# Routing's place in the order of a mixture-of-experts kernel, three weight loads, one turned block and the engines of the last two splits

## The chip, the cores and the metric

One core of a Trainium2 chip runs one program. The time is device microseconds of that core, the median of 3 runs. Engines: PE is TensorE, DVE is VectorE, ACT is ScalarE, POOL is GpSimd, SP is SyncE, whose queue issues nearly all transfers. Each engine works through its own list of instructions in order.

## The reference

Three steps follow each other. The input is 2304 tokens of 512 numbers (4 sequences of 576 positions, 8 heads of 64), all in float32.

```python
# 1 retention
scores = scale * np.matmul(q, k.transpose(0, 1, 3, 2))
out = np.matmul(scores * Dmat, v)              # Dmat: causal, gamma ** distance
# 2 mixture of experts, the best 2 of 8
noisy_logits = x @ w_gate + np.log1p(np.exp(x @ w_noise)) * noise
top2 = np.argpartition(-noisy_logits, 2, axis=1)[:, :2]
h = np.maximum(x[mask] @ w1[e], 0.0)           # 512 -> 1024
out[mask] += top2_w[mask, k, None] * (h @ w2[e])
# 3 feed-forward, 512 -> 2048 -> 512
h = x @ w_in
return ((h * np.cos(h)) @ w_out).astype(np.float32)
```

## The kernel before

**Float32 products in three passes.** Weights and activations are split into a high part `h` (rounded by ACT) and a low part `l` (the difference, by DVE or POOL), and a product is h·h + l·h + h·l (`PASSES`). Weights come as *units* of 128 x 1024 floats, 512 KB each. `load_unit` (L285) puts one transfer of a unit into SP's queue, into one of three staging tiles `st`. `split_unit` (L298) makes the high part on ACT (L308) and the low part on DVE or POOL (L309), and then calls `load_unit` for the next one. Units 0 to 3 are the first layer of expert 0, 4 to 7 its second layer.

**Stage A** (loop at L1000, 20 tiles of 128 tokens). Step `j` loads the q, k and v of tile j + 4 (1 MB), has POOL multiply q by the decay for tile j + 2 (`decay`, L449, `qt<-qr`), computes the scores of tile j + 1 (L475, L484), the outputs of tile j (L498 to L517) and the gate of tile j - 1, and writes the tile's rows to the buffer `xs` in DRAM (L543). From step 3 on (`WJ`), one unit of expert 0's first layer is split in each step.

**Routing** runs as generators in four groups of tiles (`routing`, L608). A generator yields after every operation or two. It computes softplus, the top 2 and a one-hot matrix on DVE (up to L671, `mm`), then running counts on PE (L678 to L687, the *ranking*), then for each tile two one-hot pairs on DVE (L718, L719) that PE multiplies into `ptab` (L710), a table of which token goes to which place of which expert. After the last group `rank_experts` (L565) sorts the experts by size: PE L579 and L580, then a chain on DVE from L740 to L751. The order also tells which expert's weights come next.

**Stage B.** While the last two groups are routed, PE computes expert 0 on its first 352 places, which were gathered from the first two groups alone: `layer1` (L892, 8 chunks of 12 matmuls) and `layer2` (L913, 4 chunks of 24, in two PSUM banks in turn; DVE turns each finished chunk into `y`, L918). The order is fixed when the program is built, by a planner of a few lines. It keeps two estimated clocks, `P` for the array's matmuls and `D` for routing, and `pump` (L945) takes the next routing operations as long as `D` is not more than `SLACK` = 1.8 ahead of `P`:

```python
for k, _ in enumerate(post):        # a step of stage B, three or so matmuls
    spent(0.33, L_US)               # P += 0.33; D counts L_US for DVE's share
    pump()
```

Afterwards POOL gathers the remaining rows of expert 0 (L811), PE transposes them (L859), a matmul spreads the indices (L560), the engines pass a branch on overflowing experts (L1079), and `layer1` of expert 0's remaining places begins (L892).

**Expert stretch** (L1387). Experts 0 to 7 follow each other; while one is computed, POOL gathers rows for the next and `turn(e + 1, blk)` (L847) brings them into columns. For expert 1, blocks 0 and 1 are *whole-row* blocks: ACT copies the rows into the one tile `xt` (L856), PE transposes it (L859), ACT and DVE split it (L836, L837). Other blocks are turned by DVE alone (L844). Within expert 0, `TURN_AT0` says behind which step of its second layer (24 matmuls a step) each block is turned.

**Last stage** (L1442). Nine blocks of 256 tokens: `mlp1` (L1329), cosine on ACT and DVE, `mlp2` (L1358). During the first block, the last units of w_out are split; PE uses the last two, d2 and d3, at the end of `mlp2`. `turn2` (L1280) prepares the next block: ACT and DVE combine two expert outputs with their weights (L1307, L1308), DVE transposes (L844), ACT and DVE split (L836, L837).

Of the kernel before, what the change touches and what calls it, by code (L numbers as in the profile page):

```python
# [48 lines left out]
ZERO = (22, 27, 27, 29, 33, 38, 44)  # L49
LOOK = 4  # L50
WJ = 3
T0_AT = ()
SP0 = (0, 1, 3, 5, 7, 9)

# [20 lines left out]
ONE2 = 0.7  # L75
MARK2 = -0.5
B_US = 1.1
L_US = 0.04
OP_US = 0.21
ONE_US = 0.7  # L80
MARK_US = 0
# [1 line left out]
SPLIT_POOL = False  # L83
L1_WAIT = 2
B_AT = (0, 5, 10, 24)
TURN_AT0 = (1, 1, 2, 3, 4)
GN = max(z - a for a, z in GRP)
EARLY_N = GRP[EARLY - 1][1] // NC * S + GRP[EARLY - 1][1] % NC * 128
MID = N // 2
# [127 lines left out]
def moe_kernel(ctx, tc, x, out, dbg=None, phases="ABC"):  # L217
    nc = tc.nc
# [12 lines left out]
    state = {}  # L231
# [33 lines left out]
    units = []  # L265
# [19 lines left out]
    def load_unit():  # L285
        u = state["load"]
        if u >= len(units):
            return
        if u // 8 < E and u // 8 not in expert:
            state["owed"] += 1  # L290
            return
        state["load"] += 1
        st = stage.tile([128, 1024], F32, name="st")
        src = units[u][1]
        nc.sync.dma_start(st, src() if callable(src) else src)
        loaded[u] = st

    def split_unit(lo_engine=nc.vector):  # L298
        u = state["split"]
        state["split"] += 1  # L300
        tag, _, shp = units[u]
        st = loaded.pop(u)
        if tag[0] == "x":
            hi, lo = (t.rearrange("p a b -> p (a b)")[:, :1024].rearrange("p (a b) -> p a b", a=DC)
                      for t in x_tiles(int(tag[1])))
        else:
            hi, lo = (state[tag[0]].tile(shp, F32R, name=k + tag) for k in "hl")
        nc.scalar.activation(hi.rearrange("p a b -> p (a b)"), st, AF.Copy)  # L308
        lo_engine.tensor_tensor(lo.rearrange("p a b -> p (a b)"), st,  # L309
                                hi.bitcast(F32).rearrange("p a b -> p (a b)"), op=OP.subtract)  # L310
        W[u] = (hi, lo)
        load_unit()


    A = ExitStack()
# [244 lines left out]
            nc.tensor.matmul(pq[:, g], state["spread"][:, g], src, start=True, stop=True)  # L560
        return pq

    ranked, begun = [0], []

    def rank_experts():  # L565

# [41 lines left out]
    def routing(gi):  # L608
# [98 lines left out]
        def table(keep, last=False):  # L707
            while len(sel) > keep:
                r, sa, sb = sel.pop(0)
                nc.tensor.matmul(ptab, sa[:r], sb[:r], start=not begun, stop=last and not sel,  # L710
                                 skip_group_check=True)
                begun.append(1)

        for c in range(n):
# [7 lines left out]
            yield "one"  # L722
            table(4)
        yield "table"
        table(0, gi == len(GRP) - 1)
        if gi == EARLY - 1:

# [88 lines left out]
    def pace(src):  # L816

        nc.gpsimd.tensor_copy(beat, src.bitcast(F32))  # L818
# [120 lines left out]
    def spent(pe, dve=0.0):  # L939

        at["P"] += pe
        if dve:
            at["D"] = max(at["D"], at["P"] + PE_LAT) + dve

    def pump():  # L945

        clock[0] += 1
        while at["D"] < at["P"] + (SLACK if l1 else SLACK2):
            for it in gens[:2] if l1 or not LASTFIRST else gens[1::-1]:
                if it[1] <= at["P"]:  # L950
                    break
            else:
                return
            m = next(it[0], "end")
            if m == "end":
                gens.remove(it)
            elif m == "wait":
                it[1] = at["P"] + 0.3
            elif m == "done" and not l1:

                gens.remove(it)
                rest.append(it)
            else:
                one, mark = (ONE_US, MARK_US) if l1 else (ONE2, MARK2)
                at["D"] = max(at["D"], at["P"]) + (one if m == "one" else OP_US)
                if m in ("rank", "table"):
                    it[1] = at["D"] + mark
                elif m == "one":
                    it[1] = at["D"] - 2 * one
# [30 lines left out]
    for j in range(-2, NTILE + 1):  # L1000
        if j >= 0:
            load_tile(j + LOOK)
        if j == WJ - 2:
            for _ in range(3):
                load_unit()
        if 0 <= j + 2 < NTILE:
            decay(j + 2)
        if j == -2:
            late = late_consts()
            next(late)  # L1010
        pump()
        tail = j % NC == NC - 1
        if 0 <= j + 1 < NTILE:
            decay_v(j + 1)
            for _ in scores(j + 1):
                spent(0.87 if (j + 1) % NC == NC - 1 else 0.5, 0.6)
                pump()
        if j >= -1:
            next(late, None)
        turn_early()  # L1020
        if 0 <= j - 1 < NTILE:
            gate(j - 1)
            spent(0.37, 0.6)
        pump()
        fill(LF[0])
        if 0 <= j < NTILE:
            outputs(j)
            spent(1.75 if tail else 2.8)
        fill(LF[1])
        pump()  # L1030
        turn_early()
        if 0 <= j - 1 < NTILE:
            gate_t(j - 1)
            spent(0.11, 0.13)
            for gi, (_, z) in enumerate(GRP):
                if z == j:
                    gens.append([routing(gi), 0])
        fill(LF[2])
        if j < NTILE:
            pump()  # L1040
        for i in range(7):
            if ZERO[i] == j:
                zero_overflow(i)
        if j >= WJ and state["split"] < 4:
            split_unit(nc.gpsimd if SPLIT_POOL else nc.vector)
            if not SPLIT_POOL:
                spent(0, 1.1)
    A.close()
# [4 lines left out]
        turned.append(1)  # L1053
    late, l1, post = [2], None, chain(l1, layer2(0, 0, True))
    for k, _ in enumerate(post):
        spent(0.33, L_US)
        pump()
        if k in T0_AT and not gens:
            turn(0, late[0])
            late[0] += 1  # L1060
        if k in B_AT:
            split_unit()
            spent(0, B_US)
        for i in range(7):
            if ZERO[i] == NTILE + k:
                zero_overflow(i)
# [304 lines left out]
    def steps(g, n):  # L1371
        for _ in range(n):
            next(g, None)
# [13 lines left out]
    for e in range(E):  # L1387
# [31 lines left out]
        for _ in chain(layer2(e, 0), layer2(e, 1)) if 0 < e < E - 1 else layer2(e, 1):  # L1419
# [7 lines left out]
            else:  # L1427
                for blk in range(NB):
                    if (TURN_AT if e else TURN_AT0)[blk] == m:
                        turn(e + 1, blk)  # L1430
# [11 lines left out]
    for i in range(len(blocks)):  # L1442
        parts = []
        n = 0
        fg = fetch(i + 1)
        for _ in mlp1(i, parts):
            if n in SP0 and state["split"] < len(units):
                split_unit()
            if not i and parts:
                pace(parts[-1][0][0:1, 0, 0:1])  # L1450
            steps(fg, 1 if i or n > 5 else 2)
            n += 1
        drain(fg)
        tg = turn2(i + 1)
        while state["split"] < len(units):
            split_unit(nc.gpsimd)
            steps(tg, 1)
        drain(tg)
        if i + 1 < len(blocks):
            mlp2(i, (0, 1), parts)  # L1460
        else:
            mlp2(i, (0,), parts)
            mlp2(i, (1,), parts, ((0, DM // 2), (DM // 2, DM)))
# [18 lines left out]
```

## Time and profile before

| what | value |
|---|---|
| median of 3 runs | 965.17 us (964.54 to 966.52) |
| the profiled execution | 963.31 us |
| its span, first to last instruction | 961.5 us |
| PE busy | 940.1 us, 98% of the span |
| DVE busy | 679.5 us, 71% |
| ACT busy | 369.4 us, 38% |
| POOL busy | 466.0 us, 48% |
| mean granted TensorE clock | 0.988 |
| transfers | 135.22 MB, 141 GB/s on average |

The profiled execution took 1.8 us longer than its span. A busy share is an average over the stages, so the views that follow are taken stage by stage: busy time by stretch, then the timeline of one engine, whose brackets give the idle time ahead of an instruction and what ended it.

### The profile page before, as it was taken

To read this page: it belongs to the slowest core of one execution; us is meant where nothing else is said; L and a number is where in the kernel's file an instruction comes from. 1 tells how busy PE (TensorE), PEld (TensorE's weight loads), DVE (VectorE), ACT (ScalarE), POOL (GpSimd) and SP (SyncE) were. 2 spreads that over 40 slices of the span, in tenths; PEclk is the share of its full clock that TensorE was granted. 3 is DMA by queue.
4 is the path that set the end of the run, shared out by engine and by line. 5 is a ranking of instruction groups with operands and counts; after the bars stand their busy time and mean duration, and the time that the engine had idled before them with its cause. 6 is when DMAs were issued, how large, how long until landed. Compare 5 with 4: busy or idle time off the path is not lost.

```text
span 961.5 us, 18173 instructions
## 1 busy us (share of the span) xinstructions
PE 940.1 (98%) x6861; PEld 881.8 (92%) x6861; DVE 679.5 (71%) x1380; ACT 369.4 (38%) x653; POOL 466.0 (48%) x537
## 2 busy tenths in 40 slices
PE   8988998999999999999999999999999999999998
PEld 6877897999999999999999997989899898989897
DVE  4789876777887868796974596838494856667571
ACT  2522412441424233232433364536253534445451
POOL 6444204561726545372811175556473737373621
PEclk9998997999999999999999999999999999999999
DMA  9988487555766767686845541010101111111110
GB/s 347 294 256 243 106 306 222 159 185 169 237 201 187 228 198 251 169 271 174 273 132 151 173 147 58 14 53 18 50 20 47 27 43 31 39 34 37 31 23 23
DMA packets 78505, 135.22 MB, mean 141 GB/s; under 512 B 12912, under 2 KB 42128, under 8 KB 78416
## 3 DMA queue, kind: packets, MB, share of 16 engines
q1 hardware_dynamic: 68992, 113.57, 38.1%
q0 software_dynamic: 9280, 20.20, 7.5%
q8 instruction: 55, 0.90, 0.4%
q10 hardware_dynamic: 144, 0.27, 0.1%
q14 instruction: 34, 0.28, 0.1%
HBM read 106.53 MB, written 34.82 MB: 147 GB/s over the span
## 4 chain that ended last, share of the span: by engine, by line
PE 77%; DVE 3%; issue 1%; POOL 1%; DMA 1%; ACT 0%; DVEq 0%; SPq 0%; POOLq 0%; ACTq 0%
PE py L1358 19%; PE ph L913 13%; PE ph L1329 10%; PE ph L892 8%; PE pt L892 7%; PE pt L1329 7%; PE pt L913 4%; PE ptab L892 4%; PE ptab L913 3%; PE ptab L1329 3%; DVE t L1336 1%; DVE lb L309 1%; DMA st<-w 1%; POOL ld L309 0%; DVE t L1337 0%
## 5 line engine op out<-in xcount | busy, mean ns | idle before, releaser
L1346 POOL TENSOR_TENSOR gl<-t,gh 128x512 fp32r<-128x512 f32 x67 | 86.9, 1298 | 136.3 <-issue 95.2
L805 POOL DMA_INDIRECT rows<-xs,gidx x132 | 134.7, 1021 | 34.0 <-issue 26.8
L1272 POOL DMA_INDIRECT y<-ys,slot x128 | 125.1, 977 | 50.7 <-DVE t L1341 22.0
L818 POOL COPY beat<-hh 1x1 f32<-1x1 f32 x120 | 44.2, 369 | 153.3 <-ACT hh L897 152.0
L913 PE MATMUL ph<-hl,hb 128*128 128x256 f32 (+8 forms) x304 | 91.1, 300 | 0.0
L913 PE MATMUL ph<-hh,lb 128*128 128x256 f32 (+8 forms) x304 | 91.0, 299 | 0.0
L913 PE MATMUL ph<-hh,hb 128*128 128x256 f32 (+8 forms) x304 | 90.7, 298 | 0.0
L1308 DVE SCALAR_TENSOR_TENSOR y<-y,wts,y 128x128 f32<-128x128 f32 x64 | 36.8, 606 | 55.7 <-DMA y<-ys,slot 48.2
L1337 DVE TENSOR_SCALAR t<-t 128x512 int32<-128x512 int32 x72 | 68.2, 947 | 2.5
L1335 DVE TENSOR_SCALAR t<-t 128x512 f32<-128x512 f32 x72 | 35.1, 488 | 47.2 <-ACT t L1334 47.2
L836 ACT ACTIVATE xh<-xt 128x512 fp32r<-128x512 f32 (+7 forms) x33 | 19.6, 593 | 115.1 <-DVE xt L844 115.1
L1340 ACT ACTIVATE t<-t,cbias 128x512 f32<-128x512 f32 x72 | 51.9, 721 | 26.8 <-DVE t L1337 25.9
L1358 PE MATMUL py<-ld,gh 128*128 128x512 f32 (+1 forms) x152 | 58.2, 383 | 2.1 <-POOL ld L309 1.9
L1358 PE MATMUL py<-hd,gh 128*128 128x512 f32 (+1 forms) x152 | 58.4, 384 | 0.0
L1358 PE MATMUL py<-hd,gl 128*128 128x512 f32 (+1 forms) x152 | 58.3, 384 | 0.0
L1358 PE MATMUL py<-hb,gl 128*128 128x512 f32 (+1 forms) x152 | 58.2, 383 | 0.0
L1358 PE MATMUL py<-hb,gh 128*128 128x512 f32 (+1 forms) x152 | 58.2, 383 | 0.0
L1358 PE MATMUL py<-lb,gh 128*128 128x512 f32 (+1 forms) x152 | 58.2, 383 | 0.0
L913 PEld LDWEIGHTS ph<-hh,hb 128*128 128x128 f32 x304 | 57.3, 189 | 0.0
L913 PEld LDWEIGHTS ph<-hl,hb 128*128 128x128 f32 x304 | 57.3, 188 | 0.0
L913 PEld LDWEIGHTS ph<-hh,lb 128*128 128x128 f32 x304 | 57.2, 188 | 0.0
L309 DVE TENSOR_TENSOR lb<-st,hb 128x1024 fp32r<-128x1024 f32 x35 | 43.7, 1247 | 12.3 <-ACT hb L308 12.3
(338 smaller groups left out, 2664.9 us busy)
## 6 DMA issues: line engine op xcount, KB each, us to landing
st<-w SPq DMA_DIRECT2D x64, 512.0 KB
kv<-kv SPq DMA_DIRECT2D x16, 512.0 KB
ci<-wi SPq DMA_DIRECT2D x16, 512.0 KB
wc<-cy SPq DMA_DIRECT2D x32, 256.0 KB
ci<-wo SPq DMA_DIRECT2D x16, 512.0 KB
st<-wc SPq DMA_DIRECT2D x16, 512.0 KB
ys<-c_zero SPq DMA_DIRECT2D x7, 1024.0 KB
qr<-qt SPq DMA_DIRECT2D x20, 256.0 KB
```

The lines of the kernel that those rows point to most:

```text
L309: lo_engine.tensor_tensor(lo.rearrange("p a b -> p (a b)"), st, hi.bitcast(F32).rearrange("p a b -> p (a b)"), op=OP.subtract)
L805: nc.gpsimd.indirect_dma_start(out=t[:, g, :], out_offset=None, in_=xs.rearrange("n (a d) -> (n a) d", a=4), in_offset=bass.IndirectOffset ...
L818: nc.gpsimd.tensor_copy(beat, src.bitcast(F32))
L892: nc.tensor.matmul(p[:, :n], w[a][:, dc, (f % 2) * 128:(f % 2 + 1) * 128], XE[e, g][b][:, dc, :n], start=(i == 0), stop=(i == 3 * DC - 1))
L913: nc.tensor.matmul(p[:, :n], w[a][:, f % 2, c * 128:(c + 1) * 128], HE[e, g][b][:, f, :n], start=(i == 0), stop=(i == 3 * FC - 1))
L1272: nc.gpsimd.indirect_dma_start(out=t[:, g, :], out_offset=None, in_=ys.rearrange("n (a d) -> (n a) d", a=4), in_offset=bass.IndirectOffset ...
L1308: nc.vector.scalar_tensor_tensor(y0[:, g], y1[:, g], w1, y0[:, g], op0=OP.mult, op1=OP.add)
L1329: nc.tensor.matmul(p[:, f, :], w[a][:, dc, f * 128:(f + 1) * 128], X2[i][b][:, dc, :], start=(k == 0), stop=(k == 3 * DC - 1))
L1337: nc.vector.tensor_scalar(t.bitcast(I32), t.bitcast(I32), 0x7FFFFFFF, None, op0=OP.bitwise_and)
L1340: nc.scalar.activation(t, t, AF.Sin, scale=-1.0, bias=cbias[:, 1:2])
L1346: (nc.gpsimd if i or g > 4 else nc.vector).tensor_tensor(fl(gl), T[g], fl(gh.bitcast(F32)), op=OP.subtract)
L1358: nc.tensor.matmul(ps_[tb][:, :c1 - c0], parts[f // 2][b][:, f % 2, tb * 128:(tb + 1) * 128], w[a][:, f % 2, c0:c1], start=(f + k == 0), s ...
```

## The change

Four edits. Stage B's planner counts 0.49 instead of 0.33 for a step of the array, and 0.1 instead of 0.04 for DVE's share of it. Units 4, 5 and 6 are no longer loaded behind the splits of steps 4 to 6 of stage A, but behind steps 12, 13 and 14 (unit 3 still behind the split of step 3). Block 1 of expert 1 is turned behind step 2 of expert 0's second layer, not behind step 1. The last two splits have their low parts on DVE and on POOL, both ahead of `turn2`, where both were on POOL with a step of `turn2` between. A wait in the generator (`tabled`) keeps the groups' last table matmuls in order.

```diff
+LATE_AT = (12, 13, 14)
...
-L_US = 0.04
+L_US = 0.1
...
-TURN_AT0 = (1, 1, 2, 3, 4)
+TURN_AT0 = (1, 2, 2, 3, 4)
...
-    def split_unit(lo_engine=nc.vector):
+    def split_unit(lo_engine=nc.vector, more=True):
...
-        load_unit()
+        if more:
+            load_unit()
...
         yield "table"
+        while tabled[0] < gi:
+            yield "wait"
+        tabled[0] += 1
         table(0, gi == len(GRP) - 1)
...
+        if j in LATE_AT:
+            load_unit()
...
-            split_unit(nc.gpsimd if SPLIT_POOL else nc.vector)
+            split_unit(nc.gpsimd if SPLIT_POOL else nc.vector, j == WJ)
...
-        spent(0.33, L_US)
+        spent(0.49, L_US)
...
-        while state["split"] < len(units):
-            split_unit(nc.gpsimd)
-            steps(tg, 1)
+        for eng in (nc.vector, nc.gpsimd):
+            if state["split"] < len(units):
+                split_unit(eng)
```

The lines of the changed kernel are numbered a little higher: L52 to L312 by 2, L313 to L724 by 3, L725 to L1040 by 6, and those behind by 8.

**PE, end of the routing in stage B, before** (`ptab<-sb,sa` is the last table matmul, L579 and L580 the counts for `rank_experts`, `py<-hh,hb` and the like are `layer2`):

```order
L710 LDWEIGHTS sa
L710 MATMUL ptab<-sb,sa 128x144
L579 LDWEIGHTS ones
L579 MATMUL ph<-run,ones 128x8
L580 LDWEIGHTS ones
L580 MATMUL ph<-adj,ones 128x8
L913 MATMUL py_2043<-hh_1656,hb_1746 128x352
L913 MATMUL py_2043<-hh_1656,lb_1747 128x352
```

**PE at the same place, changed:**

```order
L713 LDWEIGHTS sa
L713 MATMUL ptab<-sb,sa 128x144
L582 LDWEIGHTS ones
L582 MATMUL ph<-run,ones 128x8
L583 LDWEIGHTS ones
L583 MATMUL ph<-adj,ones 128x8
L919 MATMUL py_1989<-hh_1656,hb_1891 128x352
L919 MATMUL py_1989<-hh_1656,lb_1892 128x352
```

The rows read alike, but they stand in another chunk of `layer2`: 87 of its 96 matmuls were ahead of L580, and 9 behind it; now 42 are ahead and 54 behind. The first ranking moved from behind 72 of the 96 matmuls of `layer1` to behind 57, the second from behind all 96 to behind 69. On DVE, the second, third and fourth `y<-py` (L918) now all stand behind L751.

**SP's queue in stage A, steps 6 and 7, before** (`st<-w` is a weight unit, `qr`, `kb`, `kv` the three loads of a tile, `xs<-xr` the write of rows):

```order
L543 DMA xs<-xr 32x4x128 x4
L295 DMA st<-w 128x1024
L349 DMA qr<-qt 128x512
L355 DMA kb_130<-kt 128x512
```

**SP's queue behind steps 12 and 13, changed:**

```order
L546 DMA xs<-xr 32x4x128 x4
L297 DMA st<-w 128x1024
L352 DMA qr<-qt 128x512
L358 DMA kb_131<-kt 128x512
L369 DMA kv<-kv 128x1024
L546 DMA xs<-xr 32x4x128 x4
L297 DMA st<-w 128x1024
L352 DMA qr<-qt 128x512
L358 DMA kb_132<-kt 128x512
```

The units stood ahead of the loads of tiles 9, 10 and 11; now they stand ahead of the loads of tiles 17, 18 and 19.

## Rows read from the trace of the kernel before

**Rows 1.** The page, part 2: granted clock in tenths, 40 slices of 24 us.

```profile
PEclk9998997999999999999999999999999999999999
```

**Rows 2.** Stretch, its us, busy us PE, PEld, DVE, ACT, POOL; clock, DMA, GB/s.

```profile
450.00:500.00 50.00, 50.00 (x384) 50.00 (x383) 42.47 (x83) 18.26 (x32) 25.75 (x36) 1.00 0.68 203
```

**Rows 3.** The same table, a slice of stage A.

```profile
50.00:60.00 10.00, 7.32 (x80) 5.93 (x78) 8.55 (x31) 1.86 (x5) 4.29 (x5) 0.86 1.01 318
```

**Rows 4.** Timeline of PE, stage A: start, us, line, operation, [idle before <- releaser].

```profile
57.35 2.15 PE L475 MATMUL ph<-qt,kb 64*128 64x128 f32 x16 [2.68 <-DVE sa L718]
...
84.48 0.28 PE L685 MATMUL ph<-mm,ones 128*128 128x40 bf16 x5 [3.32 <-DVE mm L671]
...
92.08 1.16 PE L475 MATMUL ph<-qt,kb 64*128 64x128 f32 x16
```

**Rows 5.** Timeline of SP's queue and of POOL, stage A.

```profile
48.33 0.52 SPq L349 DMA_DIRECT2D qr<-qt  x1
...
55.99 1.31 POOL L449 TENSOR_TENSOR qt<-qr,dq 128x512 f32<-128x512 f32 x1 [5.07 <-DMA qr<-qt]
...
83.10 1.26 POOL L449 TENSOR_TENSOR qt<-qr,dq 128x512 f32<-128x512 f32 x1 [1.76 <-DMA qr<-qt]
```

**Rows 6.** Busy us as in rows 2, behind the first wait of PE.

```profile
57.35:75.00 17.65, 17.64 (x199) 14.93 (x199) 14.18 (x42) 5.40 (x15) 9.60 (x9) 0.91 0.80 227
```

**Rows 7.** Timeline of PE around the end of stage B.

```profile
113.07 0.76 PE L892 MATMUL ph<-xh,ha 128*128 128x352 f32 x3 [0.27 <-ACT xh L836]
...
145.57 0.17 PE L580 MATMUL ph<-adj,ones 128*128 128x8 bf16 x1
...
150.03 1.11 PE L859 MATMUL pt<-ident,rows 128*128 128x128 f32 x4 [2.73 <-DMA rows<-xs,gidx]
...
153.97 1.77 PE L560 MATMUL ph<-gf,spread 128*128 128x40 f32 x8
...
156.04 1.22 PE L892 MATMUL pt<-xh,ha 128*128 128x264 f32 x4 [0.30 <-PEq L1079]
...
162.32 0.65 PE L892 MATMUL ph<-xh,ha 128*128 128x264 f32 x4
```

**Rows 8.** The chain that ended last: two runs of matmuls at full clock.

```profile
162.48 4.36 PE ph L892 x36
...
620.07 22.12 PE py L1358 x96
```

**Rows 9.** Busy us by engine, stage B's routing.

```profile
114.70:145.63 30.93, 30.93 (x209) 29.21 (x207) 22.28 (x92) 7.51 (x12) 0.00 (x0) 1.00 0.76 259
```

**Rows 10.** Timeline of DVE, end of stage B.

```profile
125.97 0.19 DVE L671 TENSOR_TENSOR mm<-oh 128x32 bf16<-128x32 f32 x1
...
151.04 0.54 DVE L918 STREAM_TRANSPOSE y<-py 128x352 f32<-128x352 f32 x1
```

**Rows 11.** DMA issues: two whole-row gathers, us from issue to landing.

```profile
rows<-xs,whole POOLq DMA_INDIRECT x2, 6.5
```

**Rows 12.** Timeline of PE, expert 0's second layer.

```profile
174.31 0.66 PE L859 MATMUL pt<-ident,xt 128*128 128x128 f32 x4 [1.21 <-ACT xt L856]
```

**Rows 13.** Timeline of PE, first block of the last stage.

```profile
570.54 0.39 PE L1358 MATMUL py<-hb,gh 128*128 128x512 f32 x1
...
592.68 0.50 PE L1358 MATMUL py<-ld,gh 128*128 128x512 f32 x1 [1.92 <-POOL ld L309]
...
596.90 0.28 PE L1329 MATMUL ph<-x2h,hc 128*128 128x256 f32 x1
```

**Rows 14.** Timeline of POOL, DVE and ACT in that block.

```profile
585.28 2.40 POOL L309 TENSOR_TENSOR ld<-st,hd 128x1024 fp32r<-128x1024 f32 x1
...
590.28 2.35 POOL L309 TENSOR_TENSOR ld<-st,hd 128x1024 fp32r<-128x1024 f32 x1 [2.60 <-ACT hd L308]
...
584.00 3.85 DVE L1308 SCALAR_TENSOR_TENSOR y<-y,wts,y 128x128 f32<-128x128 f32 x4
...
594.40 0.63 ACT L836 ACTIVATE x2h<-y 128x512 fp32r<-128x512 f32 x1 [3.03 <-DVE y L844]
```

More of the change, by code (lines that the diff above doesn't have):

```diff
@@ L561, in spread_out @@
         return pq
-    ranked, begun = [0], []
+    ranked, tabled, begun = [0], [0], []
     def rank_experts():
```

## The prediction

> **What bounds the kernel now.** I read the page first: PE is busy for 98% of the span, and the slices of granted clock show only three dips, at the start, near 50 to 90 us and near 150 us [rows 1]. The table by stretch comes next. In the expert stretch PE is busy for 50.00 of 50 us at clock 1.00, while DVE has 7.5 us left over [rows 2]. So there nothing but PE sets the time, and whatever is gained ahead of it shifts all that follows. What an edit can win is PE's idle time or its time at the lower clock level, and I looked for both in PE's timeline, place by place. Four places have some, and the four edits lie at them. An idle bracket names what ended a wait; I followed each back to the queue behind it.
>
> All sums are against the profiled execution of 963.31 us, 1.86 below the median of 965.17.
>
> **Edit 1, three units later in stage A: gain 3.0.** PE waits 2.68 us ahead of the scores of tile 11 [rows 4]. The row names DVE, but that instruction also needs POOL's `qt`, and POOL had itself waited 5.07 us for the transfer `qr` and began at 55.99, to end 57.30 [rows 5], just ahead of PE's 57.35. The transfer was issued at 48.33 and so took 7.7 us to be usable. In this slice the transfers run at a full share, 1.01, and 318 GB/s [rows 3]: a 0.5 MB unit costs 0.52 / 318 GB/s = 1.6 us of it, three cost 4.7. The edit takes the unit directly ahead away, and the two ahead of that: `qr` lands 1.6 to 4.7 earlier, against a wait of 2.7. The wait also costs clock: the slice's mean is 0.86 [rows 3], and the same 16 matmuls take 2.15 us behind the wait and 1.16 elsewhere [rows 4], so 1.0 more. The ceiling is 2.68 + 0.99 = 3.7. What can withhold it is DVE, busy for 8.55 of these 10 us [rows 3]: if PE no longer waits for POOL it next waits for DVE's `sa` or `am`. Behind the wait it is busy for 14.18 of 17.65 us [rows 6], and these 3.5 are what it can give. I take 3.0, near that. The lower end is 0.
>
> The other side of the move: the same 1.5 MB now stand ahead of the loads of tiles 17 to 19. POOL's `qt` of tile 17 started at 83.10 and ended at 84.36 [rows 5], and PE used it at 92.08 [rows 4]: 7.7 us of slack, over the 4.7 that all three units cost. The units themselves are expert 0's second-layer weights, first used behind 125 us. I cost this at nothing; without that slack it is at most the 4.7. The gap of 3.32 us at 84.48 waits for DVE's `mm` [rows 4] and stays.
>
> **Edit 2, the planner's longer steps: gain 6.1.** Before, L580 stands at 145.57 with only 9 matmuls of `layer2` behind it. One such matmul costs 0.161: 36 of `layer1` with 264 columns take 4.36 at full clock [rows 8], so 0.121 each, times 352 / 264. The nine are over at about 147.1. `layer1` resumes at 156.04 [rows 7], 8.9 later. In between PE has three transposes of 1.11 us and the spread of 1.77 [rows 7], all at the lower level; at full clock half, 1.65 + 0.9. So 6.35 of the 8.9 is lost, and then 36 matmuls take 156.04 to 162.32 = 6.28 [rows 7] where full clock needs 4.36 [rows 8]: 1.9 more. The ceiling is 8.3, and 156.04 counts as 157.95 at full clock.
>
> After, 45 matmuls move from ahead of L580 to behind it: 45 x 0.161 = 7.25, so PE can reach L580 at 138.3. Can DVE? From 114.70 to 145.63 DVE is busy for 22.28 us [rows 9], and two transposes of 0.54 [rows 10] move behind; 114.7 + 21.2 = 135.9, a slack of 2.4. The second ranking is tighter. PE gets there behind 69 instead of 96 matmuls of `layer1`: 113.07 [rows 7] + 69 x 0.161 + 0.3 for the ranking's own = 124.5. DVE's `mm` ended at 126.16 before [rows 10]; with fewer operations ahead of it I put it at 124.7 to 125.7. PE waits 0.2 to 1.2; I take 0.5.
>
> Behind L580 comes the next limit. DVE's chain from L740 to L751 ran 145.63 to 151.04 (the two ends in [rows 9, 10]), 5.4 us. From 138.3 it ends at 143.7, and a `y` transpose behind it at 144.3. The fourth chunk of `layer2` needs the bank that this frees; PE is there at 138.3 + 30 x 0.161 = 143.1, waits 1.2, and ends the last 24 at 148.2. The gathers are issued behind L580 too and landed 4.5 us after it (150.03 against 145.57 [rows 7]); 6.5 at the longest median I find for a row gather [rows 11] gives 144.8. Both are under the matmuls. Then 1.65 + 0.9, and 0.6 for splits between (the brackets there are 0.3 [rows 7]): `layer1` resumes at 151.35 at full clock. 157.95 - 151.35 - 0.5 = 6.1. The lower end is 3.1, if the rest waits as it did for about half; the upper is 8.3.
>
> **Edit 3, block 1 a step later: gain 1.2.** PE waits 1.21 us for ACT's copy [rows 12]. A step of 24 matmuls, 24 x 0.121 = 2.9, now covers the copy. A unit's split comes ahead of it on ACT; if that takes the cover, 0 is left. The lower end is 0.
>
> **Edit 4, the last two splits: gain 2.9.** The first block's `mlp2` runs from 570.54 to the next block's start at 596.90 [rows 13] = 26.36, and the same 96 matmuls take 22.12 further on [rows 8]. 4.2 are lost, 4.1 without the step to the next block. The last wait, 1.92, is for POOL's second split [rows 13], which started at 590.28 after 2.60 for ACT's high part [rows 14]: that high part stood behind a step of `turn2`. Now both splits go first, d2 on DVE until about 585.3, d3 on POOL from 585.28 (when POOL began d2 before [rows 14]) to 587.7; PE needs them at about 587.4 and 590.6. The next limit is `turn2`, put back by two splits. Before, DVE's four L1308 took 3.85 beside POOL's split of 2.40, so some 1.45 alone, and ended at 587.85; the second half of the block's columns was ready at 595.03, 7.2 later [rows 14], with another four L1308 beside another split of 2.35 between. Now they end 1.45 behind POOL's one split, 589.1, and 7.2 - 2.35 = 4.8 later, at 593.9, the columns are there, where PE is free at 570.54 + 22.12 = 592.7. That costs 1.2 of the 4.1. The bounds are 2.0, with 0.9 more for a step that this chain queues behind, and 4.1.
>
> The 3.85 us read as one engine standing still for the other. The Trainium skill, page "SBUF — State Buffer", section "SBUF: two separate sides", says that the port pair of DVE and GpSimd is an exclusive lock: the first to start holds it for its whole instruction. By that rule, which speaks against putting two splits on these two engines, the sum would lose up to 1.4 (rival 3 below), where the rows alone leave DVE's split done at 585.3.
>
> **The sum.** 3.0 + 6.1 + 1.2 + 2.9 = 13.2; 963.31 - 13.2 = 950.1 profiled, and 1.86 more as a median: **952.0 us**.
>
> **Rivals.** (1) DVE bounds stage A. PE's wait moves from `qt` to `sa`, and edit 1 gives nothing. For it: the bracket names `sa` [rows 4] and DVE has only 1.45 us free in that slice [rows 3]. Against it: the 3.5 us behind [rows 6]. 955.0. (2) Edit 2 is worth half: DVE's operations, or gathers held up by transfers at a share of 0.76 [rows 9], keep PE waiting between 148 and 154. 952.0 + 3.0 = 955.0. (3) POOL's split starts before DVE's, whose 1.2 us (half of POOL's 2.40 [rows 14], an estimate) then end at 587.7 + 1.2 = 588.9, against PE's need at 587.4 less 0.1: 1.4 less gain, 953.4. For it: the 3.85 [rows 14]. By the page's rule this is what the order of starts decides. (4) The other side: slower. PE stands at the earlier rankings, waiting for DVE, long enough for the clock to fall to the lower of its levels (1.2 of 2.4 GHz), as it did behind the gap at 147 to 150 [rows 7]; then 39 matmuls of `layer1`, 42 and 54 of `layer2`, 135 in all, cost 0.161 more each: 21.7, and 952.0 + 21.7 = 973.7. It turns the sign from 82 such matmuls on (13.2 / 0.161). For it: my slack at the second ranking is below nothing. Against it: the wait is 0.5, not the 2.7 that cost clock before [rows 4]. (5) The expert stretch has another pace-maker, transfers (share 0.68 [rows 2]) or POOL, and gives back edits 1 to 3: 965.17 - 2.9 = 962.3. Against it: PE without a gap [rows 2].
>
> **Chances.** Forecast 0.55; rival 1 0.14; 2 0.13; 3 0.05; 4 0.08; 5 0.05. A measurement of this kernel can tell about 0.2% (1.9 us) from no change. All but rival 4 and half of 5 are faster by more: 0.55 + 0.14 + 0.13 + 0.05 + 0.02 = 0.89; same 0.03; slower 0.08. The range reaches from the ceilings (3.7 + 8.3 + 1.2 + 4.1 = 17.3, so 947.9; 947.5 with the spread of the runs) to rivals 1 and 2 together (958.0).
>
> **What would show it.** Edit 1: the scores of tile 11 have no wait above 0.5 us and the clock stays near 1 in 50 to 60; if a wait for `sa` or `am` stands there with DVE without a gap, rival 1. Edit 2: L583 near 135 (edit 1's 3.0 taken off 138.3), `layer1` resumed near 148.4 at clock 1, a short wait for `y` ahead of the fourth chunk. Rival 4 would show clock near 0.5 between 120 and 150. Edit 3: no idle time at the first transposes of expert 0's second layer. Edit 4: `mlp2` of the first block without a wait for `ld`, and about 1 us at the next block's start. PE below 50.00 of 50 in the expert stretch would make the whole sum wrong.

## The result, and the profile after

The changed kernel takes **956.71 us** (median of 5 runs, 953.92 to 958.0) where the kernel before took 964.54 in the same comparison: a ratio of 0.9913, 95% interval 0.9888 to 0.9938, 7.8 us less. That is faster, by an interval that excludes no change. It is inside the range of 947.5 to 958, but the forecast was a gain of 13.2, to 952.0. On another chip the same two kernels took 955.11 and 963.85 (0.9907, 0.9870 to 0.9944).

The profiled execution has a span of 954.9 us (961.5 before). The first line is the granted clock of the page, against [rows 1]; then the table by stretch, against [rows 3], for the same slice and for the routing part of stage A as a whole, 40 to 100 us, with the row of the kernel before under it (stretch, its us, busy us of PE, PEld, DVE, ACT, POOL, clock, share of the transfers, GB/s).

```profile
PEclk8998999999999999999999999999999999999999
```

```profile
50.00:60.00 10.00, 7.02 (x67) 6.02 (x67) 9.73 (x43) 1.63 (x4) 4.54 (x4) 0.83 0.93 296
...
40.00:100.00 60.00, 53.64 (x576) 44.66 (x576) 56.98 (x189) 17.96 (x44) 27.11 (x26) 0.91 0.80 242
```
```profile
40.00:100.00 60.00, 53.45 (x581) 44.43 (x579) 53.77 (x188) 17.89 (x45) 27.25 (x25) 0.91 0.81 240
```

The 7 at 144 to 168 us is gone; the 8 at 72 to 96 is still there, and a new one stands at the start, ahead of any edit. The slice from 50 to 60 is no better than it was: PE 7.02 us busy where it was 7.32, clock 0.83 where it was 0.86. What changed there is DVE, 9.73 of 10 us instead of 8.55, and over the whole routing part 56.98 of 60 instead of 53.77. Next PE's timeline, against [rows 4, 7, 13] (start, us, line, operation, and in brackets the idle time ahead and what ended it):

```profile
54.88 0.27 PE L688 MATMUL ph<-mm,ones 128*128 128x40 bf16 x5 [2.06 <-DVE mm L674]
59.16 1.16 PE L478 MATMUL ph<-qt,kb 64*128 64x128 f32 x16
64.31 0.22 PE L713 MATMUL ptab<-sb,sa 128*128 128x144 f16 x1 [0.96 <-DVE sb L722]
84.85 0.27 PE L688 MATMUL ph<-mm,ones 128*128 128x40 bf16 x5 [2.08 <-DVE mm L674]
113.97 0.75 PE L898 MATMUL ph<-xh,ha 128*128 128x352 f32 x3 [0.27 <-ACT xh L842]
139.15 0.17 PE L583 MATMUL ph<-adj,ones 128*128 128x8 bf16 x1
145.23 0.43 PE L919 MATMUL py<-hh,hb 128*128 128x352 f32 x1 [0.94 <-DVE y L924]
151.81 0.72 PE L898 MATMUL pt<-xh,ha 128*128 128x264 f32 x4 [0.30 <-DVE xl L843]
155.54 0.75 PE L898 MATMUL pt<-xh,ha 128*128 128x264 f32 x4 [2.05 <-ACTq L1087]
169.65 0.39 PE L919 MATMUL ptab<-hl,hb 128*128 128x264 f32 x1 [0.40 <-DVE hl L904]
590.22 0.74 PE L1337 MATMUL ph<-x2h,hc 128*128 128x256 f32 x4 [0.97 <-ACT x2h L842]
```

Read it place by place. Edit 1: the scores of tile 11 (59.16) have no wait, as forecast, but they start 1.8 us later than before; the wait stands a few instructions earlier, for DVE's `mm`, and another for `sb`. Edit 2: L583 at 139.15, `layer1` resumed at 151.81 at full clock, and a wait of 0.94 for `y` ahead of the fourth chunk, all within 1 us of the forecast counted from the start of stage B; then a wait of 2.05 that I had not listed, behind ACT at the branch (L1087). Edit 3: the wait for `xt` is gone. Edit 4: no wait for `ld`, and 0.97 for `x2h` at the next block.

To find what each edit is worth I divide each profile at four rows: the first `layer1` matmul of 352 columns (the start of stage B); the fourth group of expert 0's second piece (162.32 in [rows 7]); the first matmul of expert 1 (183.57 before); and the first `mlp2`, from its start to the next block's (26.36 in [rows 13]). One execution each:

| kernel | stage B starts | to the 4th group | to expert 1 | first `mlp2` |
|---|---|---|---|---|
| before | 113.07 | 49.25 | 21.25 | 26.36 |
| before, a second profile | 113.53 | 48.95 | 21.27 | 24.78 |
| changed | 113.97 | 44.60 | 20.93 | 23.24 |
| changed, a second profile | 114.81 | 44.61 | 20.18 | 23.72 |
| edit 1 undone | 113.80 | 44.63 | 19.81 | 22.12 |
| edit 2 undone | 112.68 | 49.24 | 19.85 | 22.11 |
| edit 3 undone | 107.62 | 44.62 | 21.26 | 23.29 |
| edit 4 undone | 113.37 | 46.13 | 19.82 | 23.39 |

The last stage behind that block takes 364.6 to 364.7 us in both first profiles and in the four with an edit undone. Between the first two profiles the span's 6.6 us are then: -0.9 until stage B, 4.65 and 0.3 in the next two columns, 0.3 in the expert stretch, -0.8 in the first `mlp1` (PE waits 0.69 behind an instruction of ACT that begins 3.17 us late), 3.1 in the first `mlp2`. Within kernels that have edit 2 the second column is tight, but for one row; the other three are not, and that is half of the answer.

### The profile page after: what moved, and what is told of

Read it like the earlier page. It is cut to its first block, busy times and chain, and to the rows that moved or that the text cites. A ratio compares the mean times of both kernels' runs of the same rounds, so it can differ in the third digit from the quotient of the medians.

```text
span 954.9 us, 18173 instructions
## 1 busy us (share of the span) xinstructions
PE 934.6 (98%) x6861; PEld 878.1 (92%) x6861; DVE 679.4 (71%) x1381; ACT 367.9 (39%) x653; POOL 467.3 (49%) x536
## 4 chain that ended last, share of the span: by engine, by line
PE 79%; DVE 2%; issue 1%; ACT 1%; DMA 0%; DVEq 0%; ACTq 0%
PE py L1366 19%; PE ph L919 13%; PE ph L1337 11%; PE ph L898 9%; PE pt L898 7%; PE pt L1337 7%; PE pt L919 4%; PE ptab L898 4%; PE ptab L1337 3%; PE ptab L919 3%; DVE y L1316 0%; DMA st<-wc 0%; DVE t L1344 0%; DVE la L311 0%; DVE t L1349 0%
## 5 line engine op out<-in xcount | busy, mean ns | idle before, releaser
L824 POOL COPY beat<-hh 1x1 f32<-1x1 f32 x120 | 49.7, 414 | 151.2 <-ACT hh L903 148.7
L1316 DVE SCALAR_TENSOR_TENSOR y<-y,wts,y 128x128 f32<-128x128 f32 x64 | 35.1, 582 | 55.4 <-DMA y<-ys,slot 46.6
L919 PEld LDWEIGHTS ph<-hh,hb 128*128 128x128 f32 x304 | 57.3, 188 | 0.0
```

The source lines that it names most:

```text
L919: nc.tensor.matmul(p[:, :n], w[a][:, f % 2, c * 128:(c + 1) * 128], HE[e, g][b][:, f, :n], start=(i == 0), stop=(i == 3 * FC - 1))
L1316: nc.vector.scalar_tensor_tensor(y0[:, g], y1[:, g], w1, y0[:, g], op0=OP.mult, op1=OP.add)
```

## The experiments

**Each edit undone.** The four kernels are the changed one with one edit taken back:

```diff
-        if j in LATE_AT:
-            load_unit()
-            split_unit(..., j == WJ)
+            split_unit(..., True)
```
```diff
-        spent(0.49, L_US)      # L_US = 0.1
+        spent(0.33, L_US)      # L_US = 0.04
```
```diff
-TURN_AT0 = (1, 2, 2, 3, 4)
+TURN_AT0 = (1, 1, 2, 3, 4)
```
```diff
-        for eng in (nc.vector, nc.gpsimd):
-            if state["split"] < len(units):
-                split_unit(eng)
+        while state["split"] < len(units):
+            split_unit(nc.gpsimd)
+            steps(tg, 1)
```

Expected, edit 1: 

> The changed kernel (956.7 median, its trace 954.9 span) with units 4 to 6 loaded early again, as before. Theory: stage A is paced by DVE, edit 1 only moved PE's wait from POOL's qt to DVE's mm and sb, and is worth nothing: time within 1.5 us of 956.7, the wait of some 2.7 us ahead of the scores of tile 11 is back, the waits for mm of 2.06 at the first ranking and of 0.96 for sb are gone, and layer1 of stage B begins within 1 us of 113.97. Rival (my forecast): edit 1 is worth 3.0, hidden in the changed kernel's run by a slower start; then 959.7, with layer1 at about 117.

Expected, edit 2: 

> The changed kernel with the planner's old numbers (0.33 and 0.04). From the traces, edit 2 moved the end of the first 36 matmuls of expert 0's second piece from 162.32 to 158.57 while stage B began 0.90 later, so it is worth 4.65: about 961.3. Forecast: 6.1, 962.8. Rival: part of the later start of stage B (0.9) belongs to edit 2; then layer1 of stage B begins at about 113.1 here and the loss is under 4.

Expected, edit 3: 

> The changed kernel with block 1 turned behind step 1 again. From the traces the stretch between the 36 matmuls and expert 1's first layer became only 0.3 shorter (new waits of 0.58 us for DVE's hl): 957.0. Forecast: worth 1.2, 957.9, if the 0.58 came from the earlier arrival of PE at that place and not from edit 3. Either way the wait of 1.2 for ACT's xt must be back.

Expected, edit 4: 

> The changed kernel with both last splits on POOL again. Forecast: edit 4 is worth 2.9, 959.6. By the whole stretch in the traces 2.3 (959.0), where 0.69 was lost to a wait of PE behind an ACT instruction that started 3.17 us late in the first block's mlp1. If that late start belongs to edit 4, it is not here and the first block takes 2.3 longer; if it is independent, the first block takes 2.9 longer apart from it.

Measured on one chip, with the kernel before at 962.11: edit 1 undone 953.36 (ratio 0.9916, 0.9895 to 0.9937), edit 2 undone 957.03 (0.9947, 0.9927 to 0.9967), edit 3 undone 954.88 (0.9932, 0.9908 to 0.9956), edit 4 undone 955.18 (0.9911, 0.9881 to 0.9940). Beside the changed kernel's 0.9913, undoing edit 2 moves the ratio by 0.0034, 3.3 us, with intervals that overlap from 0.9927 to 0.9938; the other three can't be told from it.

The profiles tell more. *Edit 1 undone* has the old wait back, and for the old reason. PE's timeline, then POOL's:

```profile
58.21 2.03 PE L478 MATMUL ph<-qt,kb 64*128 64x128 f32 x16 [2.85 <-DVE sb L722]
84.70 0.27 PE L688 MATMUL ph<-mm,ones 128*128 128x40 bf16 x5 [2.53 <-DVE mm L674]
113.80 0.75 PE L898 MATMUL ph<-xh,ha 128*128 128x352 f32 x3 [0.27 <-ACT xh L842]
```
```profile
56.89 1.26 POOL L452 TENSOR_TENSOR qt<-qr,dq 128x512 f32<-128x512 f32 x1 [4.88 <-DMA qr<-qt]
```

POOL's `qt` ends at 58.15 and PE goes on at 58.21. So the mechanism of edit 1 was read rightly; yet stage B starts at 113.80 with it undone and at 113.97 with it. The gain goes into the waits for `mm` and `sb`, as the theory of this experiment had it. Which leaves open why the freed time is lost there.

*Edit 2 undone* has the stretch back to 49.24 (49.25 before), so edit 2 is worth 4.6 us against the four profiles with it at 44.60 to 44.63; neither the forecast's 6.1 nor the rival's under 4. The row that falls out, 46.13 with edit 4 undone, has the same wait of 2.04 at the branch, but the clock fell behind it and did not in the others: four matmuls take 1.08 us there instead of 0.65, and 3.1 are left of the gain.

```profile
156.23 1.08 PE L898 MATMUL pt<-xl,ha 128*128 128x264 f32 x4
```

*Edit 3 undone* has its wait of 1.21 for `xt` back and 21.26 us in its stretch, against 19.82 in three others that keep the edit: it is worth 1.4. In the changed kernel's two profiles 1.1 and 0.4 of that are not had: the first has other waits there, 0.40 for DVE's `hl` among them, and in the second no single wait accounts for it.

*Edit 4 undone* was to cost 2.3 to 2.9; the time says nothing and the profile shows 23.39, where the changed kernel has 23.24. But that 26.36 of the kernel before is not here either: POOL's split is waited for 0.97 us, not 1.92 [rows 13]:

```profile
586.93 0.50 PE L1366 MATMUL py<-ld,gh 128*128 128x512 f32 x1 [0.97 <-POOL ld L311]
```

And a surprise outside all expectations: with *edit 3 undone*, whose stage A is the changed kernel's instruction for instruction, stage B starts at **107.62**. Its PE timeline:

```profile
52.17 0.27 PE L688 MATMUL ph<-mm,ones 128*128 128x40 bf16 x5 [0.65 <-DVE mm L674]
54.85 1.16 PE L478 MATMUL ph<-qt,kb 64*128 64x128 f32 x16
59.90 0.22 PE L713 MATMUL ptab<-sb,sa 128*128 128x144 f16 x1 [0.63 <-DVE sb L722]
80.14 0.27 PE L688 MATMUL ph<-mm,ones 128*128 128x40 bf16 x5 [0.77 <-DVE mm L674]
107.62 0.75 PE L898 MATMUL ph<-xh,ha 128*128 128x352 f32 x3 [0.27 <-ACT xh L842]
```

The same waits as in the changed kernel, those for `mm` a third as long. One program, 6.4 us apart in its first 114 us: that is more than any of the four edits, and goes with the times of single runs, which lie up to 8 us apart for one kernel (957.98 to 966.01 for the one before). It also shows what becomes of edit 1. In the four profiles without it (the kernel before twice, edit 1 undone, and one further down) the scores of tile 11 start at 57.3 to 59.6 us, behind a wait of 2.2 to 3.6. In the seven with this stage A none has a wait above 0.42 us there. Four of these start at 54.9 to 55.5, behind a wait of some 0.7 for `mm`, and three at 59.2 to 60.2, behind one of over 2 us and matmuls at the lower clock. So the edit does bring these scores forward, and a wait for DVE can take it back.

**What makes DVE late.** DVE's timeline in the changed kernel, and POOL's beside it:

```profile
52.98 1.60 DVE L670 TENSOR_TENSOR oh<-cs,ix 128x48 f32<-128x48 f32 x2
54.62 0.21 DVE L674 TENSOR_TENSOR mm<-oh 128x48 bf16<-128x48 f32 x1
57.35 0.90 DVE L705 CAST vf<-vq 128x24 f32<-128x24 int32 x1
```
```profile
52.25 1.26 POOL L452 TENSOR_TENSOR qt<-qr,dq 128x512 f32<-128x512 f32 x1 [3.04 <-DMA qr<-qt]
53.48 1.04 POOL L460 TENSOR_TENSOR vt<-kv,cb 128x512 f32<-128x512 f32 x1
57.17 1.05 POOL L460 TENSOR_TENSOR vt<-kv,cb 128x512 f32<-128x512 f32 x1
```

The two operations of L670 take 1.60 us here and took 0.28 in the kernel before, where POOL's were just over; they end at 54.58, POOL's two products at 54.52. Their row in the kernel before:

```profile
50.87 0.28 DVE L667 TENSOR_TENSOR oh<-cs,ix 128x48 f32<-128x48 f32 x2
```

L705 takes 0.90 instead of 0.18 and ends at 58.25, POOL's at 58.22. Each of DVE's operations that is long ends where an operation of POOL ends: from 40 to 100 us 18 of them take over 0.3 us more than the shortest of their kind, 14.8 us more in all, and each ends 0.03 to 0.07 us behind an operation of POOL. The Trainium skill, page "SBUF — State Buffer", section "SBUF: two separate sides", calls the port pair of DVE and GpSimd an exclusive lock, held for a whole instruction. The trace agrees, with these ends, for operations of SBUF on SBUF; it also shows some that are not held back: two of L480, which read PSUM, take 1.28 beside POOL's `qt` at 46.66, and a transpose 0.70 beside its product at 47.92, as elsewhere. The kernel before has the same, in DVE's timeline beside the `qt` of 55.99 to 57.30 [rows 5], just where PE waited:

```profile
56.10 1.25 DVE L718 TENSOR_SCALAR sa<-it,vf 128x128 f16<-128x128 f16 x1
```

Alone this operation takes 0.24.

I summed, for 40 to 100 us, what each of DVE's operations takes above the shortest duration of its kind (same operation on operands of the same shape) in any profile of this study; I call this DVE's excess. In the seven profiles whose stage A is the same program (the changed kernel twice, edits 2, 3 and 4 undone, and two below) the sum goes with the start of stage B: 13.4 us and 107.62, 14.5 and 109.28, 15.1 and 112.68, 16.0 and 113.37, 16.3 and 114.32, 16.8 and 113.97, 17.0 and 114.81. That is a correlation, and the granted clock goes with the start of stage B just as closely. Its mean over the first 105 us is 0.98 in the two that start first, 0.95 in the next two and 0.92 in the last three. It falls behind PE's waits, and can stay up behind short ones. The same kind of row as above from 56 to 58 us, of the changed kernel behind its wait of 2.06, and with edit 3 undone, behind one of 0.65:

```profile
56.00:58.00 2.00, 2.00 (x11) 2.00 (x11) 1.93 (x5) 0.00 (x1) 2.00 (x2) 0.50 0.96 340
```
```profile
56.00:58.00 2.00, 2.00 (x29) 1.47 (x28) 2.00 (x4) 0.50 (x2) 1.99 (x2) 1.00 1.01 298
```

So a wait for DVE can cost PE its length and some time at the lower level as well. The next kernels take away causes.

**The changed kernel again, and three single edits to it**, on one chip. The first takes the routing tails in turn, so that ACT's second tanh does not stand behind a whole tail on DVE; the second gives the product of v and its decay to ACT; the third puts both last low parts on DVE:

```diff
-        for it in rest[::-1]:
-            drain(it[0])
+        tails = [it[0] for it in rest[::-1]]
+        while tails:
+            tails = [g for g in tails if next(g, "end") != "end"]
```
```diff
-            nc.gpsimd.tensor_tensor(vt, KV[j][:, 1]..., dvv, op=OP.mult)
+            if j >= 8:
+                for h in range(H):
+                    nc.scalar.activation(vt[:, h], vr[:, h], AF.Copy, scale=dvh[:, h:h + 1])
+            else:
+                nc.gpsimd.tensor_tensor(vt, vr, ..., op=OP.mult)
```
```diff
-        for eng in (nc.vector, nc.gpsimd):
+        for eng in (nc.vector, nc.vector):
```

Expected, unaltered: 

> The changed kernel unaltered, on the chip of the next three, as their base. Theory: stage A of one and the same program ends at another time in each execution, because POOL's operations on q and v, which start when a transfer lands, hold back DVE's operations that run beside them; so layer1 of stage B begins anywhere between 107 and 114 us, and the late start of an ACT instruction in the first block (3.17 us) and the 0.58 us of waits at expert 0's second layer are not there again. Rival: these two belong to the changed program and are there again. From layer1's start to the fourth group of matmuls of expert 0's second piece it takes 44.6 us, as in three profiles so far.

Expected, tails in turn: 

> The changed kernel with the two routing tails behind rank_experts taken in turn, so that ACT's second tanh (L776) no longer stands behind the first tail's six DVE operations. Theory: PE's wait of 2.05 us behind the first 12 matmuls of expert 0's second piece is for ACT, which reaches the branch only behind that second tanh (154.68); with both tanh early, at about 153, the wait falls to 0.4 and the stretch from layer1's start to the fourth group from 44.6 to 43.0: 1.6 faster. Rival: the wait belongs to the branch itself or to the write of ys, and stays at 2.05: no change.

Expected, v's product on ACT: 

> The changed kernel with the product of v and its decay done by ACT (eight operations of 64 columns) and not by POOL for tiles 8 to 19 (those of four columns to a sequence, not the last of each). Theory: stage A is paced by DVE, and POOL's operations of 1.04 us on v are about half of what holds DVE back; DVE's excess over its shortest durations between 40 and 100 us falls from 13 to 16.5 us to about 8, and layer1 of stage B begins 2 to 4 us earlier, at 110 to 111. Rival: PE or the transfers pace stage A, or ACT's added 1.5 us per tile come into PE's way: layer1 begins at 113 or later.

Expected, both last splits on DVE: 

> The changed kernel with both of the last two low parts on DVE. Theory: POOL's split of 2.41 stops DVE's L1316 of turn2 (4.05 us for four that need 1.14 alone); with 1.22 of DVE in its place L1316 ends 1.7 us earlier, the wait of 0.97 for x2h at the next block's start is gone, and mlp2 of the first block takes 22.1 us (23.2 in the changed kernel's profile, but 22.1 in two others). Rival: DVE's second split is the new end of the chain; mlp2 waits for ld and takes 23 or more.

| kernel | median us | of before, 95% interval | stage B starts | to the 4th group | first `mlp2` |
|---|---|---|---|---|---|
| changed, again | 955.11 | 0.9907, 0.9870 to 0.9944 | 114.81 | 44.61 | 23.72 |
| tails in turn | 953.07 | 0.9894, 0.9861 to 0.9927 | 109.28 | 43.41 | 22.96 |
| v's product on ACT | 948.95 | 0.9856, 0.9819 to 0.9892 | 107.78 | 44.34 | 22.75 |
| both splits on DVE | 951.00 | 0.9869, 0.9835 to 0.9902 | 114.32 | 44.66 | 22.13 |

*Unaltered:* the instruction of ACT that began 3.17 us late in the changed kernel's first block is not late here, so that was the execution and not the program; no bracket of PE above 0.25 us is left at expert 0's second layer either. Stage B starts at 114.81, 0.8 above the top of what I had allowed.

*Tails in turn:* the wait behind 12 matmuls falls from 2.05 to 0.72. ACT's timeline of the changed kernel, that of this one, and its PE row:

```profile
154.48 0.20 ACT L776 ACTIVATE t<-d 128x4 f32<-128x4 f32 x1 [1.55 <-DVE d L775]
```
```profile
148.27 0.30 ACT L776 ACTIVATE t<-d 128x4 f32<-128x4 f32 x2 [1.65 <-DVE d L775]
```
```profile
149.66 0.75 PE L898 MATMUL pt<-xh,ha 128*128 128x264 f32 x4 [0.72 <-ACTq L1088]
```

PE went on 0.86 us after ACT's last tanh in the changed kernel (154.68 to 155.54) and 1.1 after it here (148.57 to 149.66). So PE waits for ACT to reach the branch, and ACT was kept by DVE's tail; the stretch is 1.2 shorter (1.6 expected). Why these matmuls need ACT to be at the branch was not tried.

*v's product on ACT:* the table by stretch, to be held against the changed kernel's 40 to 100 above:

```profile
40.00:100.00 60.00, 55.62 (x631) 46.55 (x632) 55.17 (x203) 36.95 (x121) 19.70 (x19) 0.97 0.83 250
```

POOL goes from 27.11 to 19.70 us busy, ACT from 17.96 to 36.95, and PE from 53.64 to 55.62 at a higher clock. DVE's excess falls to 12.0 (8 expected), and stage B starts at 107.78; the median is 6.2 us lower than the unaltered kernel's. The start of stage B proves nothing by itself, since edit 3 undone had 107.62 without this; the time does. Part of it is the clock: at a mean clock of 0.991 over the whole run the unaltered kernel's runs take 955.3 to 957.5 and this one's 952.1, at 1.000 950.4 against 945.9 and 946.8, so 3 to 5 us are there at a like clock and the rest goes with a higher one.

DVE itself was given no work and relieved of none. That POOL's results merely came sooner is not it: from 40 to 100 us the unaltered kernel's PE waits 4.3 us for DVE's `mm` and 1.0 for its `sb`, and neither PE nor DVE has a wait above 0.15 us for POOL. With v on ACT the waits for `mm` are 1.6, the one for `sb` is gone, and a new one of 1.7 is for DVE's `lg`. So the cause is shown in kind: POOL's elementwise operations hold DVE back, and DVE makes PE wait there. In size it is not: the excess fell by less than I expected, and I did not part the waits from the clock that falls behind them.

*Both splits on DVE:* DVE's timeline in the changed kernel, DVE's in this one, and PE's:

```profile
581.51 4.05 DVE L1316 SCALAR_TENSOR_TENSOR y<-y,wts,y 128x128 f32<-128x128 f32 x4
```
```profile
577.03 4.88 DVE L311 TENSOR_TENSOR ld<-st,hd 128x1024 fp32r<-128x1024 f32 x3 [1.65 <-ACT hd L310]
581.84 1.13 DVE L1316 SCALAR_TENSOR_TENSOR y<-y,wts,y 128x128 f32<-128x128 f32 x4
```
```profile
587.89 0.64 PE L1337 MATMUL ph<-x2h,hc 128*128 128x256 f32 x4
```

The four L1316 take 1.13 us where they took 4.05 beside POOL's split in the changed kernel, and PE has no wait: 22.13, full speed. Edits 1 and 2 undone had 22.12 and 22.11 without this remedy, so it is the row that shows the effect and not the total. The time's interval overlaps that of the unaltered kernel.

**Together, with and without edit 1.** The three edits at once; the same with edit 1 undone; the first with v's product on ACT from tile 4 on and also in each sequence's last tile; and the kernel before, profiled once more.

Expected, together: 

> The changed kernel with the three earlier edits together: v's product on ACT for tiles 8 to 19, the routing tails in turn, both last low parts on DVE. If they add up: layer1 at 107 to 110, 43.4 or less from there to the fourth group, 22.1 for the first mlp2; v_decay_on_act's 948.95 less 1.2 less 0.7 is 947, about 0.983 of before. Rival: with PE earlier at each place, another wait takes the gain back, and it stays at 949.

Expected, together without edit 1: 

> The same with units 4 to 6 loaded early again (edit 1 undone). Theory: with fewer operations of POOL in DVE's way the loads count again: the wait for qt ahead of the scores of tile 11 (2.8 us) is back, layer1 begins 2 to 3 us later than in three_together, and the time is about 2 us longer. Rival: edit 1 is worth nothing here too; the same time within 1 us.

Expected, all of v on ACT: 

> three_together with v's product on ACT from tile 4 on, and in every sequence's last tile too. Theory: POOL keeps only q in stage A; DVE's excess between 40 and 100 us falls under 10, the waits of PE for mm fall under 0.5, and layer1 begins about 1 us earlier than in three_together. Rival: ACT, which also makes the high parts of four units there, is late for v and PE waits for vt; layer1 begins later.

Expected, the kernel before: 

> The kernel before, once more with a profile. Its first mlp2 took 26.36 us, with a wait of 1.92 and then some nine matmuls at the lower clock; with edit 4 undone in the changed kernel it took 23.39, with a wait of 0.97. Theory: how late POOL's last split is depends on where POOL's gathers fall, so this varies from execution to execution: somewhere between 23 and 26.4. Rival: 26.4 belongs to the kernel before and is here again. Stage A: layer1 between 109 and 114.

Together they take **943.58 us** where the kernel before took 962.74 (0.9819, 0.9794 to 0.9844), against an expected 947; no other wait took the gains back. Stage B starts at 105.05, the fourth group follows 43.01 later, `mlp2` takes 22.13, and DVE's excess is 9.1. With all of v on ACT: 943.82 (0.9812, 0.9787 to 0.9837), stage B at 105.88, excess 8.6; I expected another 1 us, and there is no more to be had.

Without edit 1: 947.38 (0.9855, 0.9830 to 0.9881), 3.8 us more than with it. PE's timeline of the two, with edit 1 and without:

```profile
58.73 0.22 PE L719 MATMUL ptab<-sb,sa 128*128 128x144 f16 x1 [0.62 <-DVE sb L728]
89.07 1.16 PE L484 MATMUL ph<-qt,kb 64*128 64x128 f32 x16 [0.61 <-POOL qt L453]
105.05 0.75 PE L904 MATMUL ph<-xh,ha 128*128 128x352 f32 x3 [0.27 <-ACT xh L848]
```
```profile
57.26 1.83 PE L484 MATMUL ph<-qt,kb 64*128 64x128 f32 x16 [2.16 <-DVE sb L728]
81.96 0.27 PE L694 MATMUL ph<-mm,ones 128*128 128x40 bf16 x5 [0.73 <-DVE mm L680]
107.81 0.75 PE L904 MATMUL ph<-xh,ha 128*128 128x352 f32 x3 [0.27 <-ACT xh L848]
```

Stage B starts 2.76 us later without it, and the old wait is there (2.16). The intervals of the two ratios overlap a little, and part of the 3.8 is the clock: runs at a mean clock of 0.998 take 943.0 and 944.1 with the edit and 946.2 twice without. So edit 1 is worth some 2 to 4 us, about the 3.0 of the forecast, once DVE is less in the way, and by the times nothing while it is. The row at 89.07 has a wait of 0.61 for the `qt` of tile 18, whose load stands behind a unit. It may be the other side of the move, but this is not shown: POOL's own row there names a matmul of PE (L526) as what it waited for.

The kernel before, again, took 24.78 in its first `mlp2`, with the same wait:

```profile
592.57 0.50 PE L1358 MATMUL py<-ld,gh 128*128 128x512 f32 x1 [1.92 <-POOL ld L309]
595.22 0.64 PE L1329 MATMUL ph<-x2h,hc 128*128 128x256 f32 x4
```

In the first profile 4.22 us passed from that row to the next block [rows 13], here 2.65. So the wait is the program's and the slow matmuls behind it are not: the clock fell in one execution and not in the other. Three profiles without edit 4 give 26.36, 24.78 and 23.39, mean 24.8; the seven with it, but for those with both splits on DVE, give 23.24, 23.72, 22.12, 22.11, 23.29, 22.96 and 22.75, mean 22.9.

## Why the prediction was right, and where its sizes were not

The sign and the four places were right: PE's idle time was what could be won, and each wait that I named as the one to go did go. The sum was 13.2 and the times show 7.8. That 956.71 is inside the range is owed to its upper end, 958.0, which stood for rivals 1 and 2 together, and not to the sum. By terms:

| edit | forecast | what the profiles give |
|---|---|---|
| 1, units later | 3.0 | by the times nothing; 1.2 on the mean of seven starts of stage B against three; 2.8 beside the three later edits |
| 2, planner | 6.1 | 4.6 |
| 3, block 1 later | 1.2 | 1.4, of which single executions lose up to 1.1 |
| 4, last splits | 2.9 | 2.0 on the mean, 3.1 between the first two profiles |

*Edit 1* is the step that failed: "Behind the wait it is busy for 14.18 of 17.65 us, and these 3.5 are what it can give." I took DVE's free time as a reserve and its busy time as work. Part of it was neither: DVE's small operations last up to six times as long beside POOL's products (L702 0.99 us instead of 0.16). When loads land earlier, POOL's `qt` and `vt` move to where DVE runs the routing chain, and DVE loses what PE had won. Rival 1 named the outcome (PE's wait moves to DVE, edit 1 gives nothing, 0.14). It said nothing of why, and the reason was in front of me: I used the exclusion of DVE and POOL, with the very row that shows it, for two splits at the end of the kernel, and did not ask where else those two engines run side by side. L718 with its 1.25 us, inside the very wait of [rows 4], is the same thing.

*Edit 2*: counted from the start of stage B, the forecast had `layer1` resumed 38.8 us later; it was 37.8. The wait of 0.5 at the second ranking did not come, and the rest was 0.4 better. The failed step is the end of that sum: I stopped at the first matmul of `layer1` and let 36 follow at full clock in 4.36. They took 6.76 (151.81 to 158.57), of which 2.05 is the wait for ACT at the branch. Before, ACT was as late (158.22, PE's next group at 159.09), but 12 matmuls at the lower clock took just as long:

```profile
158.02 0.20 ACT L770 ACTIVATE t<-d 128x4 f32<-128x4 f32 x1 [1.55 <-DVE d L769]
```
```profile
159.09 0.96 PE L892 MATMUL pt<-xh,ha 128*128 128x264 f32 x4
```

What I counted as clock alone was two limits of about equal length, and only one was removed.

*Edit 3* was right in mechanism and size. *Edit 4* was right in mechanism: L1316 blocked by POOL's split, then a wait for `x2h`, forecast at 1.2: 0.48 to 1.42 in five of the seven profiles, 0.97 in the first, and none in two. Its size rested on one execution in which the clock had fallen behind the wait; 1.6 of the 4.1 us were that. Rival 3, POOL's split first, did not happen: `ld` of d2 was done in time in each profile.

Rivals 4 and 5 fell: clock 1.00 at the rankings of stage B, and PE without a gap in the expert stretch. Of rival 2 the gathers fell, with no wait above 0.25 us; its other half came in part, since the 2.05 at the branch are for ACT, which a tail of DVE's operations kept. What I had no rival for is the spread of stage A, which no single profile can show. One reading was loose, and no term hangs on it: the line of [rows 1] has two dips and not three, at 72 to 96 and at 144 to 168 us.

## What to carry to other kernels

When a wait is removed, ask what the freed engine will now run beside. Here two engines of which one holds the other back were brought together, and the gain of one load order lay idle until POOL's work went to an engine with time to spare. Before summing gains of a few us, get two profiles of one program: what differs between them is no term of the sum. And where a stretch ends at the low clock, look for a second wait of the same length underneath.

## What the runs showed of the hardware

- DVE operations between SBUF tiles, 0.16 to 0.31 us alone, took 0.7 to 1.3 us beside one of POOL's products of 1.04 to 1.27 us and ended with it; operations that read PSUM (0.68) and transposes (0.70) were not held back. Taking a quarter of POOL's work there away (27.11 to 19.70 us), with DVE's own unchanged, was worth 6.2 us of 955, 3 to 5 of them at a like granted clock.
- One and the same stage A took from 107.62 to 114.81 us, with DVE's excess from 13.4 to 17.0 and a mean granted clock from 0.98 down to 0.92 over its first 105 us.
- A branch that all engines pass let PE run 12 matmuls and then held it until 0.86 to 1.1 us after ACT's last operation ahead of it.
- The same wait of 1.92 us let the clock fall in one execution (4.22 us for the rest of the block) and not in another (2.65). So did a wait of 2.04 at the branch: four matmuls behind it took 1.08 us in one execution and 0.65 in the others.
